# Fold, weight loads and a k^T v burst moved in a linear-attention and feed-forward kernel

## The chip, the cores and the metric

The kernel runs on one core of a Trainium2 chip. The metric is the device time in microseconds (us). In the profile the engines are called PE (TensorE's matmuls), PEld (TensorE's weight loads), DVE (VectorE), ACT (ScalarE), POOL (GpSimd) and SP (SyncE, which here only issues DMAs). Every engine works through its own list of instructions in order.

## The reference

One layer: pre-norm linear attention with a "hedgehog" feature map, then a pre-norm gated feed-forward block, both with residual. S is 2048, D is 640, there are 32 heads of 20, F is 1536, and all is bf16.

```python
def _A_ref(x, wqkv, w_phi, wo):
    qkv = (x @ wqkv).reshape(B, S, 3, H, Dh).transpose(2, 0, 3, 1, 4)
    q, k, v = qkv[0], qkv[1], qkv[2]
    pq = einsum("bhsd,hdf->bhsf", q, w_phi)
    pk = einsum("bhsd,hdf->bhsf", k, w_phi)
    phi_q = concatenate([softmax(pq), softmax(-pq)], axis=-1)
    phi_k = concatenate([softmax(pk), softmax(-pk)], axis=-1)
    kv = einsum("bhsf,bhsd->bhfd", phi_k, v)
    z  = einsum("bhsf->bhf", phi_k)
    num = einsum("bhqf,bhfd->bhqd", phi_q, kv)
    den = einsum("bhqf,bhf->bhq", phi_q, z)[..., None] + 1e-6
    return (num / den).transpose(0, 2, 1, 3).reshape(B, S, D) @ wo

def _B_ref(x, w_gate, w_up, w_down):
    return (gelu(x @ w_gate) * (x @ w_up)) @ w_down

h  = x + _A_ref(layernorm(x), wqkv, w_phi, wo)
h2 = h + _B_ref(layernorm(h), w_gate, w_up, w_down)
```

## The kernel before

The 2048 rows are 16 tiles (t = 0 to 15) of 128 rows, in four blocks of four tiles. The order of every engine's instructions is the order in which the program writes them; no planner moves them.

**First stage, a loop over the tiles.** In iteration t the kernel normalises tile t + 6 and has it transposed by a DMA that SP issues into LN1T (`ln_ap`, line 167), computes pk of tile t (`k_tile`: 10 matmuls into PSUM, line 296, then two exponentials on ACT into E, line 340), projects v of tile t + 3 (`v_mm`, `v_ev`), and divides E by its sums (`k_norm`: a reduction and a reciprocal on DVE; line 355 multiplies one half of E on POOL and the other on POOL for the tiles of `VP`, else on DVE one iteration later). x W_q and w_phi are not applied one after the other: `fold` multiplies W_q with a block-diagonal w_phi beforehand, in five parts of 128 rows. For each part, 8 matmuls on PE (line 248) and one cast on ACT (line 257) write a slice of Wq2. `FQ` says at which tile each part is folded, `LQ` at which tile its transposed slice of W_q is loaded (`load_T`).

**k^T v** is summed over all tiles in one PSUM tile, kvp (`kv_tile`, 32 small matmuls for each tile of rows, line 374). The tiles are taken in four bursts: tiles 0 to 3 at t = 9 and 4 to 8 at t = 13 (`KVG`), 9 to 12 among the q groups (`KVQ`), 13 to 15 after the loop. Each burst needs both halves of E of its tiles.

**q groups.** At t = 15 the first four groups of pq follow (`q_mm`: 10 matmuls of 512 columns for a group of two, line 396; `q_exp`: two exponentials on ACT into Eq, line 401). `KVQ = {1: ...}` puts the third burst behind group 1, that is after 20 of these matmuls. Group 0 reads block 1, group 1 reads block 0. The rotating PSUM tiles of the first stage are three (four, with kvp holding one).

**Loads.** All loads and all DMA transposes of this part stand in SP's one list. W_o is loaded at the end of t = 13 (line 534). A one-column copy on POOL from Eq of group 2 into Wg (line 536) makes the load of W_gate wait: SP may issue the first four fifths of W_gate (line 538) only after it. The last fifth and W_up are issued by `load_up` (lines 553 and 554), which is called after the transpose of tile 0's attention output o has been issued. That transpose (oT, line 167) is what the first output projection, `attn_c(0)`, reads together with W_o (line 707).

**Second stage.** Attention of tiles 0 and 1 is mixed with the rest of the q groups; then `weave` mixes gate/up matmuls (line 767), down projections (line 789) and attention of the later tiles.

Of the kernel before, what the change touches and what calls it, by code (L numbers as in the profile page):

```python
# [17 lines left out]
def kernel(  # L18
# [12 lines left out]
    nc = tc.nc  # L31
# [8 lines left out]
    NC = D // P  # L40
# [6 lines left out]
    VP = (0, 2, 4, 6, 7, 9, 11, 12, 13)  # L47
    KA, QA = (0, 1, 3, 4), (0, 1, 2, 3, 4)
    LQ = (7, 8, 9, 9, 10)
    FQ = (10, 11, 12, 13, 14)  # L50

    QG = ((5, 6), (0, 1), (2, 3), (4,), (7, 8), (9, 10), (11, 12), (13, 14), (15,), (16,), (17,), (18,), (19,))
    QT = (15, 15, 15, 15)
    T3 = 3

    KVG = {9: (0, 1, 2, 3), 13: (4, 5, 6, 7, 8)}
    KVQ = {1: (9, 10, 11, 12)}
    VC = Dh + 1
    KC = Dh + 2

# [27 lines left out]
    Wg = const.tile([P, NC, FF], BF16, name="Wg")  # L88
    Wu = const.tile([P, NC, FF], BF16, name="Wu")
# [6 lines left out]
    Eq = [const.tile([P, len(g), 2, 512], BF16, name=f"Eq{j}") for j, g in enumerate(QG)]  # L96
# [14 lines left out]
    def gtile(name):  # L111
        return psG.tile([P, 2, 512], F32, name=name, tag="G")
# [87 lines left out]
    def load_T(WT, i, *ds):  # L200

        for d in ds:
            nc.sync.dma_start_transpose(WT[:, :, d * P:(d + 1) * P], A_wqkv[d * P:(d + 1) * P, i * D:(i + 1) * D])
# [3 lines left out]
    wg_v = B_w_gate.rearrange("(c p) n -> p c n", p=P)  # L207
    wu_v = B_w_up.rearrange("(c p) n -> p c n", p=P)
# [23 lines left out]
    def fold(WT, W2, quarters, ds=range(NC)):  # L232


        n, w = (2, QF) if quarters else (1, HD)
        runs = []
        for c in range(NC):
            lo, hi = H0[c] * Dh, (H0[c] + NH[c]) * Dh
            for r in range(2 * n):
                a, b = max(lo, r * w), min(hi, (r + 1) * w)  # L240
                if a < b:
                    runs.append((r // n, r, c, a, b))
        runs.sort()
        for d in ds:
            wa = gtile("wa")
            wr = wa.rearrange("p u (q x) -> p (u q) x", q=n)
            for i, (u, r, c, a, b) in enumerate(runs):
                nc.tensor.matmul(wr[:, r, a - r * w:b - r * w], lhsT=WT[:, c, d * P:(d + 1) * P],  # L248
                                 rhs=BD[:, c].rearrange("p a b -> p (a b)")[:, a - H0[c] * Dh:b - H0[c] * Dh],
                                 start=(i == 0 or runs[i - 1][0] != u),  # L250
                                 stop=(i + 1 == len(runs) or runs[i + 1][0] != u), skip_group_check=True)
            dst, src = W2[:, d, :].rearrange("p (u f) -> p u f", u=2), wr[:, :, 0:w]
            if quarters:
                dst = W2[:, d, :].rearrange("p (c r f) -> p r c f", c=NC, r=4)
                src = src.rearrange("p r (c f) -> p r c f", c=NC)
            if d in (QA if quarters else KA):
                nc.scalar.copy(dst, src)
            else:
                nc.vector.tensor_copy(dst, src)
# [15 lines left out]
    def ln_st(*tiles, act=True, between=None, log=False):  # L275
        for t, v in zip(tiles, ln_stats(p1, [x_sb[t // 4][:, t % 4, :] for t in tiles], "1", act, between, log)):
            lnp[t] = v

    def ln_ap(t, on_act=False, on_pe=False):
        ln = (ln_act if on_act else ln_dve)(p1, "1", *lnp[t])  # L280
        if on_pe:
            lnp[t] = ln
        else:
            transpose_to(LN1T[t // 4][:, :, t % 4 * P:(t % 4 + 1) * P], ln, False)
# [16 lines left out]
    def v_mm(t, us=(0, 1)):  # L301
        if 0 in us:
            pv[t] = gtile("pv")
        proj(pv[t], t, Wv, us)
# [10 lines left out]
    def v_ev(t):  # L315
        nc.scalar.activation(vS[t % NV][:, :, 1:VC].rearrange("p (u h) f -> p u h f", u=2),
                             pv[t][:, :, 0:HD].rearrange("p u (h f) -> p u h f", f=Dh), ACTF.Copy,
                             scale=lnp[t][2] if t in CT else 1.0)
# [12 lines left out]
    def k_tile(t):  # L331
        if t in pks:
            pk = pks[t]
            k_part(t, NC - 1)
        else:
            pk = gtile("pk")
            proj(pk, t, Wk2)
        Ek[t] = ev.tile([P, 2, D], BF16, name="E", bufs=10)
        for s in range(2):
            nc.scalar.activation(Ek[t][:, s, :].rearrange("p (u f) -> p u f", u=2), pk[:, :, 0:HD],  # L340
                                 ACTF.Exp, scale=((lnp[t][2], nrstd[t]) if t in CT else (1.0, -1.0))[s])

    def k_norm(t):


        sk = small(p1, [P, 2 * H], "sk")
        nc.vector.reduce_sum(sk, Ek[t].rearrange("p s (h f) -> p (s h) f", f=Dh), axis=AX.X)  # L347
        if t - 1 in todo and t < NT - 1:
            todo.pop(t - 1)()
        rs = small(p1, [P, 2 * H], "rs")  # L350
        nc.vector.reciprocal(rs, sk)  # L351

        def mult(s, eng):
            e = Ek[t][:, s, :].rearrange("p (h f) -> p h f", f=Dh)
            eng.tensor_tensor(e, e, rs[:, s * H:(s + 1) * H, None].to_broadcast([P, H, Dh]), ALU.mult)  # L355

        mult(1, nc.gpsimd)
        if t in VP:
            mult(0, nc.gpsimd)
        elif t == NT - 1:  # L360
            todo.pop(t - 1)()
            mult(0, nc.vector)
        else:
            todo[t] = lambda: mult(0, nc.vector)
# [3 lines left out]
    def kv_tile(t):  # L368

        E = Ek[t].rearrange("p s (h f) -> p s h f", f=Dh)  # L370
        for i in range(QH):
            for r in range(4):
                h = r * QH + i
                nc.tensor.matmul(kvp[QUAD[r], :, i * Dh:(i + 1) * Dh], lhsT=vF[t % NV][:, h * VC:h * VC + 32],  # L374
                                 rhs=E[:, :, h, :], start=(i == t == 0), stop=(t == NT - 1), skip_group_check=True)
# [11 lines left out]
    def q_mm(j, part=(0, 1), kcs=range(NC)):  # L387

        if 0 in part and 0 in kcs:
            pqs[j] = gtile("pq")  # L390
        for i, bc in enumerate(QG[j]):
            if i not in part:
                continue
            b, c = divmod(bc, NC)
            for kc in kcs:
                nc.tensor.matmul(pqs[j][:, i, :], lhsT=Wq2[:, kc, c * P:(c + 1) * P], rhs=LN1T[b][:, kc, :],  # L396
                                 start=(kc == 0), stop=(kc == NC - 1))

    def q_exp(j, signs=(0, 1)):
        for s in signs:  # L400
            nc.scalar.activation(Eq[j][:, :, s, :], pqs[j][:, 0:len(QG[j])], ACTF.Exp, scale=(1.0, -1.0)[s])  # L401
# [92 lines left out]
    for t in range(NT):  # L494
        if t == T3:
            kvp = gtile("kvp")[:, 0, 0:2 * QF].rearrange("p (s f) -> p s f", s=2)
        late = t in (1, 4)
        if 0 < t < NT - 6 and not late:
            ln_ap(t + 6, on_act=True)
        k_tile(t)  # L500
        if t == 0:
            ln_ap(6)
            nc.sync.dma_start(x_sb[3][:, 0:2, :], x_v[:, 12:14, :])
        if t in FQ:
            fold(WqT, Wq2, True, [i for i, f in enumerate(FQ) if f == t])
        for i in KVG.get(t, ()):
            kv_tile(i)
        for j in range(len(QT)):
            if t == QT[j]:
                q_mm(j)  # L510
                q_exp(j)
                for i in KVQ.get(j, ()):
                    kv_tile(i)
        if 0 < t < NT - 3:
            v_mm(t + 3)
        if late:
            ln_ap(t + 6, on_act=True)
        if t == 1:
            nc.sync.dma_start(x_sb[3][:, 2:4, :], x_v[:, 14:16, :])
        if 0 < t < NT - 3:  # L520
            v_ev(t + 3)
        for i in ST.get(t, ()):
            ln_st(i, i + 1)
        k_norm(t)
        load_T(WqT, 0, *[i for i, f in enumerate(LQ) if f == t])
        if t == 10:
            transpose_to(LN1T[0][:, :, P:2 * P], ln_a(1), False)
        if t == 13:
            ln_ap(0, on_act=True)
        if t == 8:  # L530
            for z in KT:
                nc.gpsimd.memset(z, 0.0)
        if t == 13:
            nc.sync.dma_start(Wo, wo_v)
    q = len(QT)
    nc.gpsimd.tensor_copy(Wg[:, 0, 0:1], Eq[q - 2][:, 0, 1, 0:1])
    for a, b in ((0, 2), (2, 4)):
        nc.sync.dma_start(Wg[:, a:b], wg_v[:, a:b])
    for t in range(13, NT):
        kv_tile(t)  # L540
    kv_mask()
# [5 lines left out]
    p2r = ctx.enter_context(tc.tile_pool(name="p2r", bufs=1, side="right", reuse_waits="tile"))  # L547
    Wd = p2r.tile([P, NF, D], BF16, name="Wd")
    wd_v = B_w_down.rearrange("(c p) n -> p c n", p=P)

    def load_up():

        nc.sync.dma_start(Wg[:, 4:NC], wg_v[:, 4:NC])
        nc.sync.dma_start(Wu, wu_v)

    def load_down(*fs):

# [279 lines left out]
    attn_b(0, True)  # L837
    attn_b2(0, True)
    attn_b3(0)
    load_up()  # L840
    attn_a(1, 0)
    q_exp(q + 1, (0,))
    q_mm(q + 2)
# [93 lines left out]
```

## Time and profile before

| | us |
|---|---|
| median of 3 runs | 272.47 |
| lowest and highest run | 272.0, 273.43 |
| the profiled execution | 272.4 |
| its span in the trace | 270.7 |
| PE busy | 265.7 (98%) |
| DVE, ACT, POOL busy | 174.9, 138.9, 101.2 |

The times in the profile are counted from the start of the span; the profiled execution took 1.7 us more than its span. PE's granted clock was 0.999 of full speed. A line of the chain of waits gives start, length and what ran. "issue" is time in which an engine waited for nothing that the profile shows. A line of a queue's timeline gives start, length, engine, line of the program, operation, output and input, and, in brackets, idle time before it and what ended it.

### The profile page before, as it was taken

How to read it: one execution, taken by the hardware profiler on the slowest of the kernel's cores; microseconds unless marked ns; L12 is line 12 of the kernel's file. 1: busy time of each engine (PE TensorE's matmuls, PEld its weight loads, DVE VectorE, ACT ScalarE, POOL GpSimd, SP SyncE). 2: the span in 40 equal slices, each digit the busy share in tenths (PEclk: the TensorE clock that was granted, in tenths of full speed). 3: DMA queues.
4: the chain of work that ended last, by engine and by line, in shares of the span. 5: the costliest groups of instructions: out<-in, count | busy, mean ns of one | idle time of the engine just before them, and what ended most of it. 6: DMA issues, size and time to landing. Idle time of an engine off the chain costs nothing.

```text
span 270.7 us, 7046 instructions
## 1 busy us (share of the span) xinstructions
PE 265.7 (98%) x2867; PEld 171.3 (63%) x2867; DVE 174.9 (65%) x347; ACT 138.9 (51%) x249; POOL 101.2 (37%) x238
## 2 busy tenths in 40 slices
PE   7999999999999999999999999999999999999995
PEld 6777777755455877788755455775555476444574
DVE  5889999996877767876466783568673332333322
ACT  5789998876789675245541356421544300322100
POOL 5548988796002335376211564014661100000000
PEclk9999999999999999999999999999999999999999
DMA  6998257250678432442201222102222101000011
GB/s 187 225 199 169 54 99 110 38 150 2 234 246 244 155 101 56 41 104 51 52 24 51 48 50 51 48 3 75 77 44 52 24 24 51 24 0 0 4 48 48
DMA packets 45264, 22.10 MB, mean 82 GB/s; under 512 B 37808, under 2 KB 43184, under 8 KB 45232
## 3 DMA queue, kind: packets, MB, share of 16 engines
q1 hardware_dynamic: 44576, 21.64, 32.6%
q8 instruction: 22, 0.36, 0.6%
q10 hardware_dynamic: 656, 0.03, 0.2%
q14 instruction: 10, 0.08, 0.1%
HBM read 10.18 MB, written 2.62 MB: 47 GB/s over the span
## 4 chain that ended last, share of the span: by engine, by line
PE 96%; DMA 2%; SPq 0%; issue 0%; DVE 0%
PE gu L767 39%; PE pd L789 19%; PE pq L396 8%; PE pk L296 8%; PE po L707 8%; PE pv L296 7%; PE kvp L374 2%; PE pv L312 2%; DMA Wv<-in_A_wqkv_dram 2%; PE ab L618 1%; PE wa L248 1%; PE ab L585 1%; PE tp L164 0%; SPq L193 0%; SPq L190 0%
## 5 line engine op out<-in xcount | busy, mean ns | idle before, releaser
L770 ACT ACTIVATE g<-gu 128x512 bf16<-128x512 f32 (+1 forms) x60 | 30.4, 510 | 73.8 <-PE gu L767 72.9
L773 DVE TENSOR_TENSOR GT<-gu,g 128x512 bf16<-128x512 f32 (+1 forms) x60 | 34.4, 580 | 46.7 <-PE gu L767 38.8
L767 PE MATMUL gu<-LN2T,Wg 128*128 128x512 bf16 (+1 forms) x300 | 61.8, 337 | 0.0
L767 PE MATMUL gu<-LN2T,Wu 128*128 128x512 bf16 (+1 forms) x300 | 61.7, 336 | 0.0
L789 PE MATMUL pd<-Wd,GT 128*128 128x320 bf16 (+4 forms) x396 | 53.9, 295 | 0.0
L789 PEld LDWEIGHTS <-GT 128*128 128x128 bf16 x396 | 37.6, 98 | 14.5 <-DVE GT L773 0.2
L767 PEld LDWEIGHTS <-Wu 128*128 128x128 bf16 x300 | 29.4, 98 | 22.6
L767 PEld LDWEIGHTS <-Wg 128*128 128x128 bf16 x300 | 29.0, 98 | 21.2
L296 PEld LDWEIGHTS <-LN1T 128*128 128x128 bf16 x290 | 27.9, 98 | 10.5
L355 POOL TENSOR_TENSOR E<-E,rs 128x640 bf16<-128x640 bf16 x25 | 31.6, 1299 | 4.4 <-DVE rs L351 4.1
L791 DVE TENSOR_TENSOR y<-pd,x_sb 128x320 bf16<-128x320 f32 (+4 forms) x33 | 15.8, 480 | 24.2 <-PE pd L789 24.2
L707 PE MATMUL po<-Wo,oT 128*128 128x320 bf16 x160 | 24.5, 299 | 0.0
L296 PE MATMUL pk<-Wk,LN1T 128*128 128x320 bf16 x160 | 24.4, 299 | 0.0
L396 PE MATMUL pq<-LN1T,Wq 128*128 128x512 bf16 x100 | 22.9, 379 | 0.0
L347 DVE TENSOR_REDUCE sk<-E 128x64 f32<-128x1280 bf16 x16 | 22.9, 1430 | 0.0
L401 ACT ACTIVATE Eq<-pq 128x1024 bf16<-128x1024 f32 (+1 forms) x26 | 19.9, 831 | 3.5 <-PE pq L396 3.3
L340 ACT ACTIVATE E<-pk 128x640 bf16<-128x640 f32 x28 | 18.7, 746 | 3.0 <-PE pk L296 3.0
L707 PEld LDWEIGHTS <-oT 128*128 128x128 bf16 x160 | 15.6, 98 | 7.3 <-ACT oT L165 0.2
L296 PE MATMUL pv<-Wv,LN1T 128*128 128x320 bf16 x130 | 19.8, 299 | 0.0
L151 ACT ACTIVATE ln<-x_sb,v,rstd 128x640 bf16<-128x640 bf16 x14 | 12.9, 920 | 13.4 <-POOL v L746 13.2
L396 PEld LDWEIGHTS <-Wq 128*128 128x128 bf16 x100 | 9.4, 98 | 10.3
L682 DVE TENSOR_TENSOR tt<-AB,w 128x1280 bf16<-128x1280 f32 x10 | 15.1, 1506 | 0.4 <-POOL w L675 0.3
(120 smaller groups left out, 290.6 us busy)
## 6 DMA issues: line engine op xcount, KB each, us to landing
out_dram<-y SPq DMA_DIRECT2D x15, 160.0 KB, 1.8
x_sb<-in_A_x_dram SPq DMA_DIRECT2D x6, 320.0 KB, 4.0
Wu<-in_B_w_up_dram SPq DMA_DIRECT2D x1, 1920.0 KB, 8.9
Wg<-in_B_w_gate_dram SPq DMA_DIRECT2D x2, 768.0 KB, 5.8
Wd<-in_B_w_down_dram SPq DMA_DIRECT2D x1, 1440.0 KB
Wo<-in_A_wo_dram SPq DMA_DIRECT2D x1, 800.0 KB, 5.2
x_sb<-in_A_x_dram SPq DMA_DIRECT2D x4, 160.0 KB, 3.3
Wv<-in_A_wqkv_dram SPq DMA_DIRECT2D x2, 320.0 KB, 4.2
```

What stands on the lines that cost most here:

```text
L296: nc.tensor.matmul(ps[:, u, 0:HD], lhsT=lnT(t, c), rhs=W[:, c, u * HD:(u + 1) * HD], start=(c == 0), stop=(c == NC - 1))
L340: nc.scalar.activation(Ek[t][:, s, :].rearrange("p (u f) -> p u f", u=2), pk[:, :, 0:HD], ACTF.Exp, scale=((lnp[t][2], nrstd[t]) if t in C ...
L347: nc.vector.reduce_sum(sk, Ek[t].rearrange("p s (h f) -> p (s h) f", f=Dh), axis=AX.X)
L355: eng.tensor_tensor(e, e, rs[:, s * H:(s + 1) * H, None].to_broadcast([P, H, Dh]), ALU.mult)
L396: nc.tensor.matmul(pqs[j][:, i, :], lhsT=Wq2[:, kc, c * P:(c + 1) * P], rhs=LN1T[b][:, kc, :], start=(kc == 0), stop=(kc == NC - 1))
L401: nc.scalar.activation(Eq[j][:, :, s, :], pqs[j][:, 0:len(QG[j])], ACTF.Exp, scale=(1.0, -1.0)[s])
L707: nc.tensor.matmul(pos[u], lhsT=st[t][:, c, :], rhs=Wo[:, c, u * HD:(u + 1) * HD], start=(c == 0), stop=(c == NC - 1))
L767: nc.tensor.matmul(gu[i][:, 0:n], lhsT=W[:, c, f * P:(f + 1) * P], rhs=LN2T[b][:, c, a0:a1], start=(c == 0), stop=(c == NC - 1))
L770: nc.scalar.activation(g[:, 0:n], gu[0][:, 0:n], ACTF.Gelu_apprx_tanh)
L773: nc.vector.tensor_tensor(st[b, "g", f][:, a0:a1], gu[1][:, 0:n], g[:, 0:n], ALU.mult)
L789: nc.tensor.matmul(pd[:, 0:f1 - f0], lhsT=st[b, "g", f][:, tl * P:(tl + 1) * P], rhs=Wd[:, f, f0:f1], start=(f == 0), stop=(f == NF - 1), ...
L791: nc.vector.tensor_tensor(y[:, f0:f1], pd[:, 0:f1 - f0], x_sb[b][:, tl, f0:f1], ALU.add)
```

## The change

Four things are moved; no arithmetic is added or removed. `FQ` folds the last part of W_q at tile 13, beside the part before it, and no longer at tile 14. The load of W_o is issued at the end of tile 5, where it was tile 13. The third burst of k^T v stands behind q group 0, where it was group 1. The copy that holds W_gate back reads the exponentials of group 0 and stands right behind them in POOL's list, which puts it ahead of the last product of tile 15; the loads of all of W_gate and of W_up follow at line 539 and 540, ahead of the transpose of tile 0's o, and `load_up` is gone. The POOL, SP and PE lists change in just these places, and on ACT the cast of part 4 of W_q now stands ahead of the layer norm of tile 0 and the exponentials of tile 14.

```diff
-    FQ = (10, 11, 12, 13, 14)
+    FQ = (10, 11, 12, 13, 13)
...
-    KVQ = {1: (9, 10, 11, 12)}
+    KVQ = {0: (9, 10, 11, 12)}
...
             if t == QT[j]:
                 q_mm(j)
                 q_exp(j)
+                if j == 0:
+                    nc.gpsimd.tensor_copy(Wg[:, 0, 0:1], Eq[j][:, 0, 1, 0:1])
                 for i in KVQ.get(j, ()):
                     kv_tile(i)
...
-        if t == 13:
+        if t == 5:
             nc.sync.dma_start(Wo, wo_v)
     q = len(QT)
-    nc.gpsimd.tensor_copy(Wg[:, 0, 0:1], Eq[q - 2][:, 0, 1, 0:1])
-    for a, b in ((0, 2), (2, 4)):
+    for a, b in ((0, 2), (2, 4), (4, NC)):
         nc.sync.dma_start(Wg[:, a:b], wg_v[:, a:b])
+    nc.sync.dma_start(Wu, wu_v)
     for t in range(13, NT):
         kv_tile(t)
...
-    def load_up():
-
-        nc.sync.dma_start(Wg[:, 4:NC], wg_v[:, 4:NC])
-        nc.sync.dma_start(Wu, wu_v)
...
     attn_b3(0)
-    load_up()
     attn_a(1, 0)
```

## The prediction

> **What bounds the kernel now.** I read the busy shares first, then TensorE's (PE's) waits, then the chain that ended last, then the queues around the edited lines.
>
> ```profile
> PE 265.7 (98%) x2867; PEld 171.3 (63%) x2867; DVE 174.9 (65%) x347; ACT 138.9 (51%) x249; POOL 101.2 (37%) x238
> ```
>
> PE is busy for 98% of the span. A busy PE need not be a full one, so its waits come next:
>
> ```profile
> PE wu L228 <- PEq L921: 0.8, 1, 0.8
> PE kvp L374 <- issue: 0.5, 1, 0.5
> PE tp L164 <- DVE xc L272: 0.4, 1, 0.4
> PE pv L312 <- DMA Wv<-in_A_wqkv_dram: 0.4, 1, 0.4
> ```
>
> Three of these waits lie in the first 9 us, which the change does not touch. Between 9 and 267 us only the second exists, 0.5 us. The change removes no matmul, so no more than about half a microsecond can be won. Everything else it can do is to make PE wait. The chain of waits shows where the half microsecond is:
>
> ```profile
> 57.20 4.32 PE pq L396 x20
> 61.52 0.97 PE kvp L374 x109
> 62.50 0.48 issue
> 62.98 0.30 PE kvp L374 x19
> ```
>
> It lies inside the third burst of k^T v, 109 matmuls in, at no tile's border, and nothing released it ("issue"). The DMA view of 60 to 63 us, in slices of 0.075 us, has a candidate:
>
> ```profile
> GB/s 410 410 410 341 341 307 205 154 321 34 34 17 0 0 0 0 0 0 0 0 0 0 0 0 0 0 0 0 0 0 0 0 0 0 0 0 0 0 0 0
> q8 instruction: 1, 0.02, 2.2%
> ```
>
> The last bytes of W_o (issued at 56.17) pass until 60.6; there one 16 KB packet of the instruction queue q8 starts (the 321). Page part 3 has 22 such packets and PE has some 5730 instructions, 260 to a packet. So q8 feeds PE, and a page that waited behind W_o would starve a burst that uses 256 instructions in 1.3 us.
>
> The queues of the moved steps are POOL's
>
> ```profile
> 54.45 10.45 POOL L355 TENSOR_TENSOR E<-E,rs 128x640 bf16<-128x640 bf16 x8 [1.63 <-DVE rs L351]
> 67.58 0.19 POOL L536 COPY Wg<-Eq 128x1 bf16<-128x1 bf16 x1 [2.68 <-ACT Eq L401]
> ```
>
> and SP's:
>
> ```profile
> 54.91 1.20 SPq L167 DMA_TRANSPOSE LN1T<-ln  x1
> 56.17 0.57 SPq L534 DMA_DIRECT2D Wo<-in_A_wo_dram  x1
> 67.80 0.89 SPq L538 DMA_DIRECT2D Wg<-in_B_w_gate_dram  x2
> 74.48 1.21 SPq L167 DMA_TRANSPOSE oT<-o  x1
> 75.74 0.57 SPq L553 DMA_DIRECT2D Wg<-in_B_w_gate_dram  x1
> 76.36 0.42 SPq L554 DMA_DIRECT2D Wu<-in_B_w_up_dram  x1
> ```
>
> POOL's eight products are E of tiles 11, 12, 13 (two each), 14 and 15 (one each). On SP, the transpose of tile 0's o now goes ahead of W_u; after the change it goes behind it.
>
> **Fold.** Part 4 of W_q moves one tile earlier: 8 matmuls, 0.33 us, with no change to PE's sum. On ACT its cast (0.57) now stands ahead of tile 0's layer norm (53.95) and E of tile 14. The norm ends near 55.5 and its transpose, 3 us at most, lands by 58.5; the q group that reads it starts at 60.7 after the change. E of tile 14 waits for pk at 55.84 instead of 55.51 and is due at DVE's reduction at 58.19. Price 0; without these covers 0.3 to 0.6.
>
> **W_o at tile 5.** SP issues it after tile 11's transpose (30.31, done 31.51). By the Wg rate below its 0.82 MB pass by 35.3, so tile 12's transpose (issued 32.90) slips about a microsecond to some 36.8, and its v matmuls start at 40.17. Price 0, with 3 us to spare. It passes ten more transposes, all later. The window 57 to 60.6 is left empty, so the page fetched at 60.6 should come earlier and the gap close. The first burst, also 128 matmuls, takes 1.32 us on the chain; this one takes 1.75. Gain if closed: 0.43.
>
> **Third burst ten matmuls earlier.** It starts at 59.36 instead of 61.52. Tile 12's matmuls follow 0.85 later, at 60.2; POOL has E of tile 12 at 54.45 + 4 x 1.306 = 59.67. It holds by 0.5 us; otherwise the lack is paid. The next q groups shift back as much, and ACT, idle 2.08 us before the third group's exponentials, takes them without a queue.
>
> **Copy on POOL.** It now reads the first q group (exponentials end at 61.34 before) and stands ahead of E of tile 15. POOL reaches it at 54.45 + 7 x 1.306 = 63.6, so it does not wait; tile 15's product ends at 65.1 instead of 64.9, while DVE's half ends at 65.58 and the last burst needs both at about 66.8. Price 0.
>
> **W_gate, W_up from 63.8.** All 3.93 MB now go in one stretch. Before, the first 1.57 MB moved so (stretch and its length in us; busy us and instructions of PE, PEld, DVE, ACT, POOL; clock; DMA share; GB/s):
>
> ```profile
> 69.00:70.00 1.00, 1.00 (x44) 0.53 (x43) 0.57 (x1) 0.00 (x0) 0.00 (x0) 1.00 0.68 135
> 70.00:71.00 1.00, 1.00 (x6) 0.43 (x5) 0.88 (x1) 0.94 (x2) 0.00 (x0) 1.00 1.04 418
> 73.00:74.00 1.00, 1.00 (x6) 0.47 (x5) 0.97 (x2) 1.00 (x2) 0.00 (x0) 1.00 0.40 148
> ```
>
> In the first 2.2 us after the issue 0.17 MB pass, then about 0.42 MB per us. After the change: 63.8 + 2.2 + 3.76/0.42 = 75.0 for the bulk. A tail follows: the second Wg half landed at 68.23 + 7.1 = 75.3, 1.9 after its bulk (73.4), with one q8 packet in between, so one engine of the 16 ran late; its bytes end near 74.6, 1.2 after the bulk. The o transpose is issued at 74.0 (74.48 less 0.43). At best it slips between: it lands 2.4 later, at 76.4, before PE's need at 76.9 (77.3 less 0.43), price 0. At worst it waits on that engine until 76.2, moves for 0.8 (its DMA share in 75 to 77) and lands 0.4 later, at 77.4: PE waits 0.5, and stands 0.1 behind its old time. So the net lies between -0.43 and +0.1. I take -0.15, the middle: the moved load is more than twice the old one, so a page fetch inside it is as likely as not to hit its end. W_gate and W_up are used only at 86.4.
>
> The sum: the profiled execution took 272.4 (span 270.7 and 1.7 around it); 272.4 - 0.15 = 272.25. The median of the runs is 272.47, 0.07 above it, so 272.3.
>
> The Trainium skill, "DMA: Bandwidth & Descriptors", section Bandwidth, says that loads from HBM are bound near 358 GB/s per core, below the 435 of the fabric. This trace differs: 412 to 428 GB/s in the Wg windows. By the page the bulk would end at 76.5, the o transpose would land at 78.9, and the sum would be 272.4 + 1.6 = 274.0.
>
> **Rivals.**
> *The gap stays (272.5).* If the missing page is not what starves the burst, the 0.48 moves with it. For it: the chain says only "issue". Against: nothing else starts or ends there. The Trainium skill, "Runtime: NRT & Kernel Launch", section Instruction fetch mechanics, speaks for it: the next 16 KiB are fetched while the present ones run, so that crossing a border is mostly hidden; by that rule the early W_o buys nothing and the time is 272.5.
> *All of it is won (272.0).* The o transpose lands in time. For it: the bulk ends only a microsecond after its issue.
> *The load is slower and PE waits for o (273.7).* W_d, with shorter rows, moved at 348 to 387 GB/s from 87 to 90. At 0.37 MB per us the bulk ends at 76.2, the tail at 77.4, and o lands at 78.6, 1.3 behind PE's old 77.3: 272.4 + 1.3 = 273.7. It decides where the tail is met at less than 0.42. Against: both Wg and Wu kept 396 to 428.
> *The page comes no earlier, but the burst does (slower, up to 274.5).* If the fetch at 60.6 hangs on a fixed time and not on W_o, its page is usable at 62.98 as now, while the burst, begun 2.16 earlier, reaches the same place near 60.4: the wait grows from 0.48 to about 2.6, net +2.1, 274.5. It decides once the page is usable later than 60.9. For it: between that fetch's start and the burst's restart lie 2.4 us, so the fetch must start by 58.0 for the gap to close entirely. Against: the fetch starts just as W_o's bytes end.
>
> **How the numbers follow.** Forecast 0.45; gap stays 0.20; all won 0.15; slow load 0.08; page late 0.07; something not seen, such as a slip in the norms' transposes, 0.05. The lower end is 272.0 less the 0.47 by which the lowest of three runs lies below their median, 271.5; the upper end is the slow load, 273.7. This leaves out the late page and half the unseen. Half a percent is 1.36 us, about what a measurement of this kernel can tell from no change (three runs span 1.43). Faster by that: no case gives it, 0.02 for scatter. Slower: the late page and a little of the slow load, 0.08. Within: 0.90.
>
> **What would show it.** Right: in the chain the third burst stands between two pieces of ten q matmuls with no "issue" in it; no instruction packet after 60 us before the burst's end; W_gate is issued near 63.8; PE waits at most 0.5 for the o transpose near 77; after that no new PE wait. Wrong: a PE wait of over a microsecond in the third burst or at L707, or one at the v matmuls of tile 12, or W_gate issued after 65.

## The result and the profile after

The changed kernel takes 272.73 us (median of 18 runs, 272.48 to 273.7); the kernel before, run beside it, 272.03 (18 runs, 271.5 to 273.43). The ratio is 1.0025, 95% interval 1.0014 to 1.0036: slower by 0.7 us, where 0.15 us faster was forecast. The three runs shown beforehand had a median of 272.47, so the base was 0.44 too high as well.

The profiled execution took 272.49, its span is 270.8. The page's part 1 and PE's waits:

```profile
PE 265.2 (98%) x2851; PEld 171.4 (63%) x2867; DVE 173.9 (64%) x347; ACT 138.9 (51%) x249; POOL 101.2 (37%) x238
```

```profile
PE wu L228 <- PEq L917: 0.8, 1, 0.8
PE po L704 <- DMA oT<-o: 0.4, 1, 0.4
PE pv L312 <- DMA Wv<-in_A_wqkv_dram: 0.3, 1, 0.3
PE kvp L374 <- issue: 0.2, 1, 0.2
```

Sixteen matmul records are missing in this trace (2851 of 2867). One that is missing between q matmuls shows as 0.05 us of "issue" in a chain and means nothing. New is the second line: the first output projection waits for the DMA transpose of o. The burst's wait is still there, at half its size. The chain at both places, first before, then after:

```profile
66.62 0.87 PE kvp L374 x96
...
72.82 4.86 PE pq L396 x22
77.68 0.68 PE po L707 x5
...
86.37 3.38 PE gu L767 x30
```

```profile
59.17 1.07 PE kvp L374 x120
60.24 0.22 issue
60.46 0.23 PE kvp L374 x8
...
66.19 0.87 PE kvp L374 x96
...
72.78 1.26 PE pq L396 x6
74.04 3.58 DMA oT<-o
77.63 0.05 issue
77.67 0.85 PE po L704 x5
...
86.51 3.38 PE gu L764 x30
```

From the fourth burst's start to the first gate/up matmuls PE now needs 86.51 - 66.19 = 20.32 us; before it was 86.37 - 66.62 = 19.75. That is the price of the o transpose: 0.57 us. The wait table shows 0.4 of it; the first five matmuls of the projection take another 0.17 more than before (0.85 instead of 0.68). In the nine other profiles in which PE waits nowhere in this stretch, it takes 19.73 or 19.74 us. The third burst takes 1.52 us (59.17 to 60.69), where it took 1.76 before.

The instruction packet in the DMA view of 57 to 60 us (slices of 0.075 us; the 218 is at 58.2):

```profile
GB/s 198 239 191 165 69 11 0 0 0 0 0 0 0 0 0 0 218 0 0 0 0 0 0 0 0 0 0 0 0 0 0 0 0 0 0 0 0 0 0 0
q8 instruction: 1, 0.02, 1.9%
```

It starts 2.4 us earlier than in the profile before, with no load beside it, and the burst still runs dry: it resumes 2.2 us after the packet's start. POOL and SP:

```profile
54.23 8.63 POOL L355 TENSOR_TENSOR E<-E,rs 128x640 bf16<-128x640 bf16 x7 [1.64 <-DVE rs L351]
62.81 0.78 POOL L513 COPY Wg<-Eq 128x1 bf16<-128x1 bf16 x1
63.55 1.86 POOL L355 TENSOR_TENSOR E<-E,rs 128x640 bf16<-128x640 bf16 x1
```

```profile
63.62 1.40 SPq L539 DMA_DIRECT2D Wg<-in_B_w_gate_dram  x3
65.06 0.56 SPq L540 DMA_DIRECT2D Wu<-in_B_w_up_dram  x1
74.04 1.20 SPq L167 DMA_TRANSPOSE oT<-o  x1
```

The copy does not wait, but takes 0.78 us instead of 0.19; the loads go out at 63.62. What moves around the o transpose, in windows of 1 us (PE, PEld, DVE, ACT, POOL busy; clock; DMA share; GB/s):

```profile
73.00:74.00 1.00, 1.00 (x6) 0.48 (x5) 0.97 (x3) 1.00 (x3) 0.00 (x0) 1.00 1.05 409
75.00:76.00 1.00, 1.00 (x6) 0.43 (x5) 0.97 (x3) 1.00 (x2) 0.00 (x0) 1.00 1.86 146
76.00:77.00 1.00, 1.00 (x6) 0.39 (x4) 0.97 (x2) 1.00 (x2) 0.00 (x0) 1.00 0.28 54
```

The bulk ends at 75, as worked out. Then most of the transpose passes (478 small packets and 8 of the load's from 75 to 76), and a remnant of both trickles on to 77 (192 small packets and 4 of the load's from 76 on). The transpose lands 3.6 us after its issue; before it took 2.4.

### The profile page after: what moved, and what is told of

The parts are those of the page before. It is cut to its first block, busy times and chain, and to the rows that moved or that the text cites. A ratio compares the mean times of both kernels' runs of the same rounds, so it can differ in the third digit from the quotient of the medians.

```text
span 270.8 us, 7029 instructions
## 1 busy us (share of the span) xinstructions
PE 265.2 (98%) x2851; PEld 171.4 (63%) x2867; DVE 173.9 (64%) x347; ACT 138.9 (51%) x249; POOL 101.2 (37%) x238
## 4 chain that ended last, share of the span: by engine, by line
PE 95%; DMA 3%; issue 1%; SPq 0%; DVE 0%
PE gu L764 38%; PE pd L786 19%; PE po L704 8%; PE pk L296 8%; PE pq L396 7%; PE pv L296 7%; PE kvp L374 2%; PE pv L312 2%; DMA Wv<-in_A_wqkv_dram 2%; PE ab L615 1%; DMA oT<-o 1%; PE wa L248 1%; PE ab L582 1%; PE tp L164 0%; SPq L193 0%
```

## The experiments

Theory Q: the o transpose stands behind W_up in the one DMA queue, and PE waits for it. Theory G, the page theory: the burst behind group 0 reaches the border of an instruction page before that page is there. Each variant ran beside the kernel before, and ratios are to it. The gap is the "issue" wait inside the third burst; landing is counted from the issue of the transpose; the stretch runs from the fourth burst's start to the first gate/up matmuls.

**Is it the o transpose?** e1 takes the late part of the loads back:

```diff
-    for a, b in ((0, 2), (2, 4), (4, NC)):
+    for a, b in ((0, 2), (2, 4)):
         nc.sync.dma_start(Wg[:, a:b], wg_v[:, a:b])
-    nc.sync.dma_start(Wu, wu_v)
...
     attn_b3(0)
+    nc.sync.dma_start(Wg[:, 4:NC], wg_v[:, 4:NC])
+    nc.sync.dma_start(Wu, wu_v)
     attn_a(1, 0)
```

> The changed kernel, with the last fifth of W_gate and all of W_up issued behind tile 0's o transpose again. Theory Q (the o transpose queues behind W_up on the engine that runs late): the transpose lands 2.4 us after its issue instead of 3.6, PE's wait at the first output projection falls from 0.4-0.6 us to 0, and the time falls by 0.5 to 0.7 us below the changed kernel, to the kernel before or up to 0.2 below it. Rival G (the burst behind group 0 meets its instruction page late in most executions, and that costs the time): no change from the changed kernel, about 0.7 us above the kernel before.

Measured: 272.31 against 271.80, ratio 1.0015 (1.0002 to 1.0028). The transpose lands after 2.4 us and the wait is gone, but 0.4 us stays, and a gap of 0.39 us stands in the burst. Both theories hold a part.

e4 does only that part of the change, in the kernel before (the copy read from group 0, all of W_gate and W_up behind it):

> The kernel before, with only the copy read from q group 0 and all of W_gate and W_up issued behind it (W_o, the fold and the burst stay). Theory Q: the bulk of the load ends near 75, the o transpose lands 3.5 us or more after its issue at 74.5, PE waits 0.2 to 0.6 us at the first output projection, 0.3 to 0.6 us slower than the kernel before. Rival G: no wait at the projection that is longer than before, no change.

Measured: 272.75 against 271.80, 1.0032 (1.0021 to 1.0044), more than expected. There is no gap in its burst; the chain shows the whole price at the projection:

```profile
66.42 0.87 PE kvp L374 x96
...
74.27 4.04 DMA oT<-o
78.30 0.05 issue
78.35 0.85 PE po L709 x5
```

The stretch to the first gate/up (87.18) is 20.76, 1.01 above 19.75. In this profile the loads alone cost more at the projection than in the changed kernel; in the times the two cannot be told apart (1.0032 and 1.0025, with overlapping intervals).

e6 asks how much load it takes: two fifths of W_up ahead of the transpose, three behind.

```diff
-    nc.sync.dma_start(Wu, wu_v)
+    nc.sync.dma_start(Wu[:, 0:2], wu_v[:, 0:2])
...
     attn_b3(0)
+    nc.sync.dma_start(Wu[:, 2:NC], wu_v[:, 2:NC])
     attn_a(1, 0)
```

> The changed kernel with only two fifths of W_up ahead of tile 0's o transpose and three fifths behind it. Queue theory: the bulk ahead of the transpose ends near 72 instead of 75, late engine included by 74.2, so the transpose lands 2.4 to 2.6 us after its issue, and PE's wait at the first output projection is 0 to 0.1; what stays is the burst's gap, so the time is that of the kernel with W_up wholly behind the transpose (0.4 us above the kernel before), about 0.3 below the changed kernel. If any load in flight ahead of it delays the transpose regardless of size: the wait stays at 0.4 to 0.6.

Measured: 272.34 against 271.98, 1.0015 (1.0007 to 1.0024), landing 2.4 us after the issue, no wait, a gap of 0.51 in the burst. A load that ends in time costs the transpose nothing.

e7 goes the other way and drops the copy on POOL, so that the loads go out some 6 us earlier:

```diff
-                if j == 0:
-                    nc.gpsimd.tensor_copy(Wg[:, 0, 0:1], Eq[j][:, 0, 1, 0:1])
```

> The changed kernel without the copy on POOL, so that W_gate and W_up are issued right behind tile 0's layer-norm transpose, near 57, and their bulk ends near 68.5. Queue theory: the transpose of o meets no load, lands 2.4 us after its issue, no wait of PE at the first output projection. Page theory: the packet that starts at 58.3 now shares its engine with the load, so it comes later or takes longer, and the gap in the burst grows from 0.2-0.4 us to 0.5-2. In sum between 0.5 us faster and 1.5 slower than the changed kernel; the trace tells the two apart.

The transpose again lands after 2.4 us without a wait, as Q says. The packet was not delayed by the load (it starts at 58.9, 0.9 us ahead of the burst, and takes its usual 0.9) and the gap is 0.39, at the low end; the load's first bytes pass only from 58.4, so this says little about a load at its full rate. The time is 272.66 against 271.98, 1.0035 (1.0017 to 1.0052). The gap explains about half of that; the profiled execution also waited 0.9 us for W_v at the start, in code that is the same in all. The rest stays open.

**Is it the burst?** e3 moves only the burst, in the kernel before (KVQ = {0: ...}):

> The kernel before, with only the third burst of k^T v behind q group 0 (W_o stays at tile 13). If W_o's bytes hold up the page: the burst needs it 2.2 us earlier, the packet still starts near 60.6, and the wait in the burst grows from 0.5 to 1.5-2.6 us: 1 to 2 us slower than before. If the page follows PE's own progress: the packet comes earlier with the burst, the wait stays at 0.2 to 0.5, no change. Theory Q says nothing here.

Measured: 272.57 against 271.80, 1.0023 (1.0004 to 1.0043).

```profile
59.82 1.06 PE kvp L374 x119
60.88 0.19 issue
61.07 0.23 PE kvp L374 x9
```

The gap is at matmul 119 of 128, as in the changed kernel at 120, where the profile before had it at 109. Between them lie the 10 q matmuls by which the burst was moved: the place is fixed in PE's list, not in the burst. The packet starts at 57.9 here and takes 1.7 us beside W_o's first bytes (3.6% of 16 engines in 3 us). So it does not hang on a fixed time. The wait, 0.19, is about what the second theory gave, but the time rose, where that theory expected no change.

e2 moves only W_o to tile 5:

> The kernel before, with only the load of W_o moved to tile 5. If W_o's bytes hold up the instruction page: the packet of queue q8 that starts at 60.6 us starts at 58 to 59, the 0.48 us of 'issue' in the third burst goes, and the time falls by 0.4 us. If the page does not depend on W_o: the packet stays at 60.6, the wait stays, no change.

Measured: 271.70 against 271.80, 0.9996 (0.9986 to 1.0005): no gap, and no gain. e8 explains why. It is the kernel before once more:

> The kernel before, unchanged, once more: a second profile, and a measure of what no change looks like. If the 0.48 us gap in the third burst belongs to every execution, it is here again. If it comes only when the instruction packet happens to be held up behind W_o, the packet starts near 58 to 59 here, there is no gap, and the span is 0.3 to 0.5 us below 270.7.

Measured: 271.82 against 271.98, 0.9997 (0.9984 to 1.0009), span 270.1.

```profile
61.61 1.13 PE kvp L374 x128
```

The packet starts at 58.8 and the burst runs through in 1.13 us. So the gap in the first profile belonged to that execution: of five profiles with the burst behind group 1 (the kernel before twice, e2, e4, e9) it is the only one that has it. Why its packet came 1.8 us later than in e8, with W_o issued at the same time, no run shows.

**Is it the page's border?** e5 moves the burst as e3 does and shortens PE's list ahead of it with the same number of warm-up columns, `warm(*[512] * 9)` for `warm(*[512] * 2, *[P] * 28)`:

> The kernel before with the third burst behind group 0, and the 30 warm-up matmuls at the start replaced by 9 with the same 4608 columns, so that PE's list is 42 instructions shorter ahead of the burst. Page theory (the gap is PE running dry at the border of an instruction page, which always lies at the same place in PE's list): the border moves from matmul 119 of the burst to 12 matmuls behind its end, the 0.2 to 0.4 us of 'issue' goes, and the time falls by 0.3 to 0.6 us against the same move with the border left in place (272.57 there), to the kernel before. Rival (the burst waits for E or is slow behind group 0 for another reason): the gap stays at matmul 119 or at a tile's first matmul, and the time stays.

The gap is gone (burst 1.13 us), the time is not: 272.61 against 271.98, 1.0033 (1.0018 to 1.0048). The shorter warm-up list cost its own: in the trace the first burst starts at 40.09, where it starts at 38.86 in the kernel before and at 39.31 at the latest in all profiles with the old list. The same flaw spoils the times of e10 and e11, which use `warm(*[512] * 6, *[P] * 12)` on e1 and on the changed kernel:

> The changed kernel with the last fifth of W_gate and W_up behind the o transpose, the burst left behind group 0, and the 30 warm-up matmuls replaced by 18 with the same 4608 columns: PE's list is 24 instructions shorter ahead of the burst, so the page border falls 3 or 4 matmuls into group 1. Page theory: the 0.4 us gap at matmul 120 goes, PE has 0.7 us of q matmuls in hand at the border, and the time falls by 0.3 to 0.4 us against the same kernel with the border inside the burst (272.31 there), to the kernel before; if the shorter warm-up costs time in the first 25 us, the trace shows that part by itself. Rival: the gap stays.

> The changed kernel, all of it, with the same 18 warm-up matmuls, so that the page border leaves the burst. If the o transpose behind W_up sets a floor: the gap goes, PE reaches the first output projection 0.2 to 0.4 us earlier and waits that much longer there (0.8 to 1.0 instead of 0.6 counted from the last q matmul), and the time stays at the changed kernel's, about 0.7 us above the kernel before. If the two costs add: the time falls by 0.2 to 0.4 us.

e10: no gap, no wait for o, 272.72 against 272.35, 1.0009 (0.9996 to 1.0022), with the first burst 0.9 us later than in e1. e11: no gap, a stretch of 20.83 to the first gate/up, 273.51 against 272.35, 1.0048 (1.003 to 1.0067).

e12 moves the border without touching the start. It is e1 with tile 8 of k^T v in another place:

```diff
-    KVG = {9: (0, 1, 2, 3), 13: (4, 5, 6, 7, 8)}
-    KVQ = {0: (9, 10, 11, 12)}
+    KVG = {9: (0, 1, 2, 3), 13: (4, 5, 6, 7)}
+    KVQ = {0: (9, 10, 11, 12), 2: (8,)}
```

> The changed kernel with the last fifth of W_gate and W_up behind the o transpose, the burst behind group 0, and tile 8 of k^T v moved from the second burst to behind group 2 (same matmuls, PE's sum unchanged, nothing touched before 52 us). 64 of PE's instructions leave the stretch ahead of the third burst, so the page border falls 24 matmuls behind its end. Page theory: no gap in the burst, and the time falls by 0.3 to 0.4 us against the same kernel with the border inside (272.31 against 271.8 before), to within 0.1 us of the kernel before. Rival (the burst's place costs time by itself): 0.3 to 0.5 above the kernel before, with or without a gap.

```profile
59.30 1.13 PE kvp L374 x128
60.43 4.42 PE pq L396 x20
64.85 0.31 PE kvp L374 x32
...
66.35 0.86 PE kvp L374 x96
...
86.08 3.38 PE gu L763 x30
```

No gap, no wait (86.08 - 66.35 = 19.73), and 272.03 against 271.90, 1.0005 (0.9994 to 1.0016): the level of before. Against e1, 0.1% or about 0.3 us; the intervals of the two overlap, so what shows the step is the traces. All in all, the six profiles with the burst behind group 0 and the border inside (the changed kernel twice, e1, e3, e6, e7) have bursts of 1.48 to 1.80 us, and the five with the border outside (e5, e10 to e13) 1.13.

The packet's lead tells the two places of the burst apart. Behind group 0 the packet starts 1.9 to 2.0 us before PE reaches the border (the changed kernel twice, e1, e6, e7) and PE runs dry; in e3 the lead is 3.0, but the packet takes 1.7 us instead of 0.9. Behind group 1 it starts 3.3 to 5.0 us before the 109th matmul in the four profiles without a gap, and 1.9 in the first, which has one. The 10 q matmuls by which the two differ take 2.2 us.

**Are those all?** e9 keeps the fold, the early W_o and the early four fifths of W_gate, and takes the other two moves back:

> The changed kernel with two of its moves taken back: the burst stands behind group 1, and the last fifth of W_gate and W_up behind the o transpose. What stays of the change is the fold at tile 13, W_o at tile 5 and four fifths of W_gate from group 0. If the two moves are the whole cost: no gap in the burst (the page is usable 1 us or more before its border), o lands after 2.4 us, and the time is that of the kernel before, within 0.1%. If the fold or W_o costs something: it is left here, 0.2 us or more above the kernel before.

Measured: 272.07 against 272.35, 0.9993 (0.9981 to 1.0005). What is left of the change costs nothing that can be measured. Its profile, its slowest execution at 272.77, shows a wait of 0.8 us for the LN2T transpose, which is issued behind W_up and lands after 4.0 us, where it took 3.0 in the kernel before: in the old order too, a transpose can meet that load.

**Do the two costs add?** e14 is the changed kernel again, e13 the changed kernel with tile 8 moved as in e12:

> The changed kernel, all of it, with tile 8 of k^T v behind group 2. Floor theory (o lands 14.0 us after the first issue of W_gate whatever PE does): no gap in the burst, PE comes 0.3 us earlier to the first output projection and waits that much longer (1.0 to 1.2 instead of 0.8, counted as the time from the fourth burst's start to the first weight load of po, less the 10.75 it takes without a wait), and the time stays at the changed kernel's. If the costs add: 0.3 us below the changed kernel.

> The changed kernel, unchanged, on the same chip, as the level for the two others: 0.5 to 0.8 us above the kernel before; gap of 0.2 to 0.5 us in the burst; o landing 14.0 us after the first issue of W_gate; wait at the first output projection 0.4 to 0.9.

Measured against 271.90: e13 272.81, 1.0028 (1.0019 to 1.0036); e14 272.98, 1.0033 (1.0019 to 1.0048). In e13's chain the gap is gone and the price at the projection is larger:

```profile
66.30 0.87 PE kvp L374 x96
...
74.14 3.80 DMA oT<-o
77.94 0.04 issue
77.99 0.85 PE po L704 x5
```

Its stretch to the first gate/up (86.83) is 20.53, 0.78 above the old; e14's is 20.37, 0.62 above. So 0.16 of the gap's 0.63 us (1.76 against 1.13) was taken back by a longer wait in these two executions, which fits costs that mostly add; in the times, 0.17 us of difference is inside the intervals. For a floor speaks that from the first issue of W_gate to o's landing it is 14.0 us in the changed kernel (63.62 to 77.62), 14.05 in e4, 14.1 in e11, 13.95 in e13 and 14.3 in e14, while o's transpose was issued 10.0 to 10.7 us after W_gate. The runs do not decide between the two.

No version beats the kernel before: the intervals of e2, e9, e10 and e12 all hold 1.

## Why the prediction was wrong

*The bound* was read rightly: PE is full, nothing but waits can change, and both costs are new PE waits.

*W_gate, W_up from 63.8.* The working gave the issue (63.62 measured), the bulk's end (75) and, at the worst end, a landing at 77.4 with PE waiting 0.5. Measured: 77.62 and 0.57. The first step that failed is "I take -0.15, the middle": the wait was taken as likely as not, and it came every time. In all five profiles with all of W_up issued ahead of the transpose from about 64 us on, the transpose landed 3.6 to 4.1 us after its issue, and in all the others after 2.4, also in e7, where W_up had gone out 16 us ahead of it. Even the worst end was too low: in e4 the stretch grows by 1.01 us. The load ran at 390 to 422 GB/s in the windows from 66 to 74, so the slow-load rival (0.37 MB per us) is not what happened; the wait came from the tail.

By the Trainium skill, "DMA: Bandwidth & Descriptors", section Bandwidth, the HBM side binds at about 358 GB/s per core; the section also calls this the share when both cores of a pair are streaming. This trace, of one core, does not show that limit: 409 GB/s from 73 to 74.

*W_o at tile 5.* The cover held and the move costs nothing (e9). The second step that failed is "Gain if closed: 0.43": there was nothing to close. One profile had the gap, and I took it for every execution's; the profiles of e8, e2, e4 and e9 have none. The base held the same gap: the profiled execution's 272.4 less 0.48 is 271.9, near the 272.03 of 18 runs. Whether the three runs' median had it too, no run shows.

*Third burst ten matmuls earlier.* E of tile 12 was in time, as worked out. The price of 0 was wrong: alone it is 0.23% (e3), and 0.15% beside the other moves (e1). The mechanism stood under the rivals, as a late page, with 0.07 and a decision point of 60.9. The page was usable at 60.46, before that point, and the burst still lost, since the point was reckoned from a base with the gap in it. The same rival says that "the fetch must start by 58.0 for the gap to close entirely". That held: it started at 58.2, and 0.22 stayed open.

By the Trainium skill, "Runtime: NRT & Kernel Launch", section Instruction fetch mechanics, the crossing is mostly hidden. That agrees with the bursts behind group 1, four out of five of which show no gap, and not with those behind group 0 that have the border inside, six out of six of which do.

*Fold and copy.* Price 0 held (e9), although the copy took 0.78 us. "3 us at most" for the layer norm's transpose was too short a bound, as the longest in the profile before landed after 4.4 us; by that, 59.9, it would still have been ahead of 60.7.

*The chances.* 0.90 for a change within half a percent was right. That 272.73 is inside the range is in part luck: the upper end was the price of the slow load, which did not come. The sign was wrong, because of the two terms that were uncertain one was a gain of 0.43 that was not there, where the burst loses about 0.4 (e1, e6), and the other was taken at its middle, where PE pays 0.57 and more.

## What to carry to other kernels

When PE is full, look for what each move could make it wait for, and take the pessimistic end where the working for it has a mechanism: a small transfer that PE needs soon, issued behind several microseconds of weights in one queue, lands after them. A burst of tiny matmuls can eat its instructions faster than a page comes (here 256 in 1.13 us, and 2.3 us from a packet's start to its use); where it stands relative to the page's border is part of its price. Profile the kernel before twice before a gap in one profile is booked as something to win.

## What was not expected of the hardware

In six of the seven profiles with a gap, PE resumes at the page border 2.3 to 2.4 us after the start of the 16 KB packet (58.2 to 60.46 after, 60.6 to 62.98 before), while the packet itself takes 0.9 to 1.1 us (1.9% of 16 engines in 3 us is 0.9). In e3 it is 3.2 us, with a packet of 1.7. From the packet's end it is 1.3 to 1.5 us in all seven. Behind group 0 the burst reaches its border 1.07 us after its start, so the packet has to start some 1.3 us before the burst.

A load that runs at 400 GB/s ends sharply for most of its bytes and late for the rest: in the changed kernel the rate falls at 75, and 12 of the load's large packets still pass between 75 and 77, the last four of them after 76, among 192 small packets of the transpose, at 54 GB/s in all. The transpose lands only behind these. Two packets of instructions fall into that load, and I suspect that they hold one engine back. Their number does not decide it: in e4 and e14 only one falls into the load, and the landing is 4.0 and 3.6 us. No run separates this from other reasons.
